# Grouped-query attention on a KV cache, one core: kv heads taken in pairs, a hand-written order, one load queue, the output weights last

## The chip, the core and the metric

The kernel runs on one NeuronCore of a Trainium2 chip. Its engines are PE (TensorE, matmuls), DVE (VectorE), ACT (ScalarE), POOL (GpSimd) and SP (SyncE, which here only issues transfers). Each runs its own instructions in order and waits for others by semaphores; 16 DMA engines move data between HBM and the on-chip memory SBUF. PE writes its results to PSUM, a memory of eight banks, from which DVE or ACT take them. The metric is device time in microseconds, the median of several runs.

## The reference

```python
B, Sq, D = 8, 4, 512
Hq, Hkv, Sk, Dh = 32, 8, 2048, 128
# x [B,Sq,D], k_cache and v_cache [B,Hkv,Sk,Dh], wq [D,Hq*Dh], wo [Hq*Dh,D], all bf16
rep = Hq // Hkv                                   # 4 query heads share a kv head
q = (x @ wq).reshape(B, Sq, Hq, Dh).transpose(0, 2, 1, 3)
k = jnp.repeat(k_cache, rep, axis=1)
v = jnp.repeat(v_cache, rep, axis=1)
scores = jnp.einsum("bhqd,bhkd->bhqk", q, k) * (Dh ** -0.5)
p = _softmax(scores, axis=-1)
o = jnp.einsum("bhqk,bhkd->bhqd", p, v)
return o.transpose(0, 2, 1, 3).reshape(B, Sq, Hq * Dh) @ wo
```

K and V are 33.55 MB each, wq and wo 4.19 MB each, x and the output 32 KB each. Every byte of K and V is used once.

## The kernel before

A *group* is one kv head of one batch: 64 groups, heads inside batches (L73). K of a group is 512 KiB and lies in SBUF as 128 partitions of 16 consecutive keys each, one row of 4 KiB per partition (`k_int`, L84 to 88); V likewise (`v_sb`, L89 to 93). K goes out on SP's queue, V on ACT's. `wo` is loaded in four pieces of 1 MiB, rows of 1 KiB, on SP's queue among the loads of groups 8, 24, 40 and 56 (L94 to 100); `wq` in four pieces ahead of all K.

For each group, PE transposes K in 16 blocks of 128 x 128 (`trans_a` L105, `trans_b` L111). The eight blocks of each half go to one PSUM tile, `kT_a` or `kT_b`, of which there is one buffer each (L49); ACT copies the first half and DVE the second into `kT_sb`. Then 16 matmuls with a block of `kT_sb` as stationary operand and the 16 queries of the group (4 heads x 4 positions) as moving operand give the scores `sT` (L154), ACT's exponential writes the probabilities `pT` (L162), 16 matmuls with V accumulate `oT_ps` (L171), one matmul of a matrix of ones with all 256 columns of `pT` gives the sums `lcs` (L179), and DVE reduces, inverts and multiplies into `oT_all` (L180 to 187). There is no maximum taken before the exponential.

The query projection (L128 to 142, 128 matmuls, 32 small ACT copies) stands ahead of the loop. For the last batch, each group is followed by the four matmuls of its heads with `wo` (L195), which accumulate `out_ps`; at the end DVE casts it and SP stores it. The code is written group by group, with K's transposition one group ahead and loads two groups ahead; a scheduler orders each engine's instructions from that, so loads run further ahead than the code has them.

Of the kernel before, what the change touches and what calls it, by code (L numbers as in the profile page):

```python
# [1 line left out]

# [7 lines left out]
BF16 = mybir.dt.bfloat16  # L10
FP32 = mybir.dt.float32
EXP = mybir.ActivationFunctionType.Exp


@with_exitstack
def kernel(
# [17 lines left out]
    NQ = rep * Sq  # L34
    KCH = Sk // 128
    DCH = D // 128
    NG = B * Hkv
    scale = float(Dh) ** -0.5
    assert Dh == 128 and Sk % 128 == 0 and D % 128 == 0
    half = Sk // 2  # L40
    hch = KCH // 2
# [4 lines left out]
    ktpool = ctx.enter_context(tc.tile_pool(name="ktpool", bufs=3))  # L46
    ppool = ctx.enter_context(tc.tile_pool(name="ppool", bufs=3))
    setup_sb = ctx.enter_context(tc.tile_pool(name="setup_sb", bufs=1))
    psum_k = ctx.enter_context(tc.tile_pool(name="psum_k", bufs=1, space=bass.MemoryType.PSUM))  # L49
    psum_s = ctx.enter_context(tc.tile_pool(name="psum_s", bufs=2, space=bass.MemoryType.PSUM))  # L50
    psum_a = ctx.enter_context(tc.tile_pool(name="psum_a", bufs=2, space=bass.MemoryType.PSUM))

    ident = const.tile([128, 128], BF16, name="ident")
    make_identity(nc, ident[:])
    ones128 = const.tile([128, 128], BF16, name="ones128")
    nc.vector.memset(ones128[:, :], 1.0)

    xT_sb = const.tile([128, DCH, T], BF16, name="xT_sb")
    qT_all = const.tile([128, B, Hq, Sq], BF16, name="qT_all")
    oT_all = const.tile([128, Hq, T], BF16, name="oT_all")  # L60
    out_sb = const.tile([T, D], BF16, name="out_sb")
    wo_sb = const.tile([128, Hq, D], BF16, name="wo_sb")
    l_bc = const.tile([128, NQ], FP32, name="l_bc")
    recip_bc = const.tile([128, NQ], FP32, name="recip_bc")

    x_sb = setup_sb.tile([T, D], BF16, name="x_sb")
    nc.sync.dma_start(x_sb[:, :], x.flatten_outer_dims())
    wq_sb = setup_sb.tile([128, DCH, HqDh], BF16, name="wq_sb")
    for dk in range(DCH):
        eng = nc.sync  # L70
        eng.dma_start(wq_sb[:, dk, :], wq[dk * 128 : (dk + 1) * 128, :])

    groups = [(b, g) for b in range(B) for g in range(Hkv)]  # L73
    woq = [int(NG * (i + 0.5) / DCH) for i in range(DCH)]

    vt = [None] * NG
    kint = [None] * NG
    kts = [None] * NG
    kta = {}
    ktb = {}  # L80

    def dma_group(gi):
        b, g = groups[gi]
        k_int = kpool.tile([128, KCH, Dh], BF16, tag="k_int", name="k_int")  # L84
        nc.sync.dma_start(
            out=k_int[:, :, :],
            in_=k_cache[b, g].rearrange("(p c) d -> p c d", c=KCH),
        )
        v_sb = vpool.tile([128, KCH, Dh], BF16, tag="v_sb", name="v_sb")  # L89
        nc.scalar.dma_start(  # L90
            out=v_sb[:, :, :],
            in_=v_cache[b, g].rearrange("(p c) d -> p c d", c=KCH),
        )
        if gi in woq:  # L94
            wi = woq.index(gi)
            hs = Hq // DCH
            nc.sync.dma_start(
                wo_sb[:, wi * hs : (wi + 1) * hs, :],
                wo[wi * hs * 128 : (wi + 1) * hs * 128, :].rearrange("(h p) j -> p h j", p=128),
            )  # L100
        kint[gi] = k_int
        vt[gi] = v_sb
        kts[gi] = ktpool.tile([128, Sk], BF16, tag="kT_sb", name="kT_sb")

    def trans_a(gi):  # L105
        ka = psum_k.tile([128, half], BF16, tag="kT_a", name="kT_a")
        for c in range(hch):
            nc.tensor.transpose(ka[:, c * 128 : (c + 1) * 128], kint[gi][:, c, :], ident[:, :])  # L108
        nc.scalar.copy(out=kts[gi][:, :half], in_=ka[:, :])  # L109

    def trans_b(gi):  # L111
        kb = psum_k.tile([128, half], BF16, tag="kT_b", name="kT_b")
        for c in range(hch):
            nc.tensor.transpose(  # L114
                kb[:, c * 128 : (c + 1) * 128], kint[gi][:, hch + c, :], ident[:, :]
            )
        nc.vector.tensor_copy(out=kts[gi][:, half:], in_=kb[:, :])  # L117

    dma_group(0)
    trans_a(0)  # L120
    trans_b(0)
    dma_group(1)

    for dk in range(DCH):
        xtp = psum_a.tile([128, T], BF16, tag="aux", name="xtp")
        nc.tensor.transpose(xtp[:, :], x_sb[:, dk * 128 : (dk + 1) * 128], ident[:T, :T])
        nc.vector.tensor_copy(out=xT_sb[:, dk, :], in_=xtp[:, :])
    for h in range(Hq):  # L128
        psq = psum_a.tile([128, T], FP32, tag="aux", name="psq")
        for dk in range(DCH):  # L130
            nc.tensor.matmul(  # L131
                psq[:, :],
                lhsT=wq_sb[:, dk, h * 128 : (h + 1) * 128],
                rhs=xT_sb[:, dk, :],
                start=(dk == 0),
                stop=(dk == DCH - 1),
            )
        nc.scalar.mul(  # L138
            out=qT_all[:, :, h, :],
            in_=psq[:, :].rearrange("d (b s) -> d b s", b=B),  # L140
            mul=scale,
        )

    out_ps = psum_a.tile([T, D], FP32, tag="outp", bufs=1, name="out_ps")

    for gi in range(NG):
        b, g = groups[gi]
        kT_sb = kts[gi]
        v_sb = vt[gi]
        q_grp = qT_all[:, b, g * rep : (g + 1) * rep, :].rearrange("d h s -> d (h s)")  # L150

        sT = psum_s.tile([128, KCH * NQ], FP32, tag="sT", name="sT")
        for c in range(KCH):
            nc.tensor.matmul(  # L154
                sT[:, c * NQ : (c + 1) * NQ],
                lhsT=kT_sb[:, c * 128 : (c + 1) * 128],
                rhs=q_grp,
                start=True,
                stop=True,
            )  # L160
        pT = ppool.tile([128, KCH * NQ], BF16, tag="pT", name="pT")
        nc.scalar.activation(out=pT[:, :], in_=sT[:, :], func=EXP)  # L162
        if gi + 2 < NG:
            dma_group(gi + 2)
        if gi + 1 < NG:
            trans_a(gi + 1)
            trans_b(gi + 1)

        oT_ps = psum_a.tile([128, NQ], FP32, tag="aux", name="oT_ps")
        for c in range(KCH):  # L170
            nc.tensor.matmul(  # L171
                oT_ps[:, :],
                lhsT=v_sb[:, c, :],
                rhs=pT[:, c * NQ : (c + 1) * NQ],
                start=(c == 0),
                stop=(c == KCH - 1),
            )
        lcs = psum_a.tile([128, KCH * NQ], FP32, tag="aux2", bufs=1, name="lcs")
        nc.tensor.matmul(lcs[:, :], lhsT=ones128[:, :], rhs=pT[:, :], start=True, stop=True)  # L179
        nc.vector.tensor_reduce(  # L180
            out=l_bc[:, :],
            in_=lcs[:, :].rearrange("p (c q) -> p q c", c=KCH),
            axis=mybir.AxisListType.X,
            op=mybir.AluOpType.add,
        )
        nc.vector.reciprocal(recip_bc[:, :], l_bc[:, :])  # L186
        nc.vector.tensor_tensor(  # L187
            out=oT_all[:, g * rep : (g + 1) * rep, b * Sq : (b + 1) * Sq],
            in0=oT_ps[:, :].rearrange("d (h s) -> d h s", h=rep),
            in1=recip_bc[:, :].rearrange("d (h s) -> d h s", h=rep),  # L190
            op=mybir.AluOpType.mult,
        )
        if b == B - 1:
            for h in range(g * rep, (g + 1) * rep):
                nc.tensor.matmul(  # L195
                    out_ps[:, :],
                    lhsT=oT_all[:, h, :],
                    rhs=wo_sb[:, h, :],
                    start=(h == 0),
                    stop=(h == Hq - 1),  # L200
                )

    nc.vector.tensor_copy(out=out_sb[:, :], in_=out_ps[:, :])
    nc.sync.dma_start(out=out.flatten_outer_dims(), in_=out_sb[:, :])

# [29 lines left out]
```

## Time and profile before

| | us |
|---|---|
| median of 3 runs | 212.43 |
| lowest and highest run | 211.34, 213.15 |
| span of the profiled execution | 210.1 |
| PE busy in it | 154.8 |
| DVE busy | 96.9 |
| ACT busy | 91.1 |

The profiled execution has its span on the page (first to last instruction) and no other time of its own; a run's time also holds what lies around the span, so spans are compared with spans and the difference to the median is added at the end. PE, DVE, ACT rows are instruction time; matmuls overlap, so PE's busy time is no sum of their lengths. The chain of waits follows the work that ended last back through what released each step:

```profile
DMA 63%; PE 24%; DVE 6%; ACT 3%; issue 2%; ACTq 1%; DVEq 0%
```

"issue" there is time in which an engine waited for nothing that the profile shows, and ACTq and DVEq are the engines' sequencers.

### The profile page before, as it was taken

To read this page: it belongs to the slowest core of one execution; us is meant where nothing else is said; L and a number is where in the kernel's file an instruction comes from. 1 tells how busy PE (TensorE), PEld (TensorE's weight loads), DVE (VectorE), ACT (ScalarE), POOL (GpSimd) and SP (SyncE) were. 2 spreads that over 40 slices of the span, in tenths; PEclk is the share of its full clock that TensorE was granted. 3 is DMA by queue.
4 is the path that set the end of the run, shared out by engine and by line. 5 is a ranking of instruction groups with operands and counts; after the bars stand their busy time and mean duration, and the time that the engine had idled before them with its cause. 6 is when DMAs were issued, how large, how long until landed. Compare 5 with 4: busy or idle time off the path is not lost.

```text
span 210.1 us, 7459 instructions
## 1 busy us (share of the span) xinstructions
PE 154.8 (74%) x3300; PEld 133.0 (63%) x3300; DVE 96.9 (46%) x262; ACT 91.1 (43%) x161; POOL 0.7 (0%) x6
## 2 busy tenths in 40 slices
PE   0000584878885877978888888898788888899981
PEld 0000574778884776968788777677777777777750
DVE  1000141235774443355665666566456665545532
ACT  0002353655352425436656555454545445664430
POOL 1000000000000000000000000000000000000000
PEclk9999996797998566589999999999699999999999
DMA  6999999999999999999999999999999999930000
GB/s 231 421 425 418 420 422 416 408 407 414 416 413 402 402 404 404 404 421 416 415 416 417 416 417 416 411 417 420 416 417 417 413 416 417 402 152 3 5 0 6
DMA packets 23296, 76.04 MB, mean 362 GB/s; under 512 B 2208, under 2 KB 6368, under 8 KB 22752
## 3 DMA queue, kind: packets, MB, share of 16 engines
q1 hardware_dynamic: 14048, 42.01, 49.8%
q10 hardware_dynamic: 9216, 33.56, 39.4%
q8 instruction: 25, 0.41, 0.7%
q14 instruction: 7, 0.06, 0.1%
HBM read 75.53 MB, written 0.03 MB: 360 GB/s over the span
## 4 chain that ended last, share of the span: by engine, by line
DMA 63%; PE 24%; DVE 6%; ACT 3%; issue 2%; ACTq 1%; DVEq 0%
DMA v_sb<-in_v_cache_dram 36%; DMA k_int<-in_k_cache_dram 21%; DMA wo_sb<-in_wo_dram 6%; PE kT_b L114 5%; PE sT L154 5%; PE kT_a L108 5%; DVE kT_sb L117 4%; PE out_ps L195 4%; PE oT_ps L171 3%; ACT pT L162 2%; ACT kT_sb L109 1%; ACTq L90 1%; PE lcs L179 1%; DVE l_bc L180 1%; DVE recip_bc L186 0%
## 5 line engine op out<-in xcount | busy, mean ns | idle before, releaser
L117 DVE COPY kT_sb<-kT_b 128x1024 bf16<-128x1024 bf16 x64 | 44.1, 689 | 77.3 <-PE kT_b L114 65.2
L109 ACT COPY kT_sb<-kT_a 128x1024 bf16<-128x1024 bf16 x64 | 64.6, 1009 | 8.4 <-PE kT_a L108 6.9
L114 PE MATMUL kT_b<-ident,k_int 128*128 128x128 bf16 x512 | 52.7, 233 | 10.9 <-DVE kT_sb L117 7.3
L162 ACT ACTIVATE pT<-sT 128x256 bf16<-128x256 f32 x64 | 24.5, 384 | 76.3 <-PE sT L154 32.3
L114 PEld LDWEIGHTS <-k_int 128*128 128x128 bf16 x512 | 38.8, 104 | 17.9 <-issue 12.6
L171 PEld LDWEIGHTS <-v_sb 128*128 128x128 bf16 x1024 | 34.7, 98 | 22.5 <-issue 22.4
L171 PE MATMUL oT_ps<-pT,v_sb 128*128 128x16 bf16 x1024 | 35.7, 170 | 16.7 <-ACT pT L162 14.8
L108 PE MATMUL kT_a<-ident,k_int 128*128 128x128 bf16 x512 | 44.9, 235 | 3.9 <-DMA k_int<-in_k_cache_dram 3.9
L180 DVE TENSOR_REDUCE l_bc<-lcs 128x16 f32<-128x256 f32 x64 | 26.9, 421 | 23.9 <-PE lcs L179 23.4
L154 PE MATMUL sT<-qT_all,kT_sb 128*128 128x16 bf16 x1024 | 37.2, 171 | 0.7 <-ACT kT_sb L109 0.4
L154 PEld LDWEIGHTS <-kT_sb 128*128 128x128 bf16 x1024 | 33.1, 98 | 6.0 <-ACT kT_sb L109 3.6
L108 PEld LDWEIGHTS <-k_int 128*128 128x128 bf16 x512 | 33.1, 105 | 4.1 <-DMA k_int<-in_k_cache_dram 4.1
L179 PE MATMUL lcs<-pT,ones 128*128 128x256 bf16 x64 | 18.4, 287 | 0.8 <-DVE oT_all L187 0.8
L131 PE MATMUL psq<-xT_sb,wq_sb 128*128 128x32 bf16 x128 | 6.7, 183 | 15.0 <-DMA wq_sb<-in_wq_dram 14.9
L186 DVE RECIPROCAL recip_bc<-l_bc 128x16 f32<-128x16 f32 x64 | 16.2, 253 | 2.2
L131 PEld LDWEIGHTS <-wq_sb 128*128 128x128 bf16 x128 | 5.5, 102 | 16.0 <-DMA wq_sb<-in_wq_dram 15.4
L187 DVE TENSOR_TENSOR oT_all<-oT_ps,recip_bc 128x16 bf16<-128x16 f32 x64 | 11.1, 174 | 3.1 <-PE oT_ps L171 0.9
L138 ACT ACT_TABLE_LOAD x1 | 1.3, 1283 | 19.7 <-DMA v_sb<-in_v_cache_dram 19.7
L195 PE MATMUL out_ps<-wo_sb,oT_all 128*32 128x512 bf16 x32 | 8.3, 382 | 1.0 <-DVE oT_all L187 1.0
L138 ACT ACTIVATE qT_all<-psq 128x32 bf16<-128x32 f32 x32 | 4.9, 202 | 7.5 <-PE psq L131 7.3
L179 PEld LDWEIGHTS <-ones 128*128 128x128 bf16 x64 | 6.2, 97 | 0.0
L195 PEld LDWEIGHTS <-oT_all 128*32 128x32 bf16 x32 | 2.4, 95 | 3.7 <-DVE oT_all L187 1.2
(11 smaller groups left out, 3.0 us busy)
## 6 DMA issues: line engine op xcount, KB each, us to landing
v_sb<-in_v_cache_dram ACTq DMA_DIRECT2D x64, 512.0 KB, 9.9
k_int<-in_k_cache_dram SPq DMA_DIRECT2D x64, 512.0 KB, 9.9
wq_sb<-in_wq_dram SPq DMA_DIRECT2D x4, 1024.0 KB, 10.3
wo_sb<-in_wo_dram SPq DMA_DIRECT2D x4, 1024.0 KB, 14.7
x_sb<-in_x_dram SPq DMA_DIRECT2D x1, 32.0 KB, 2.1
out_dram<-out_sb SPq DMA_DIRECT2D x1, 32.0 KB, 1.5
```

What stands on the lines that cost most here:

```text
L108: nc.tensor.transpose(ka[:, c * 128 : (c + 1) * 128], kint[gi][:, c, :], ident[:, :])
L109: nc.scalar.copy(out=kts[gi][:, :half], in_=ka[:, :])
L114: nc.tensor.transpose(kb[:, c * 128 : (c + 1) * 128], kint[gi][:, hch + c, :], ident[:, :])
L117: nc.vector.tensor_copy(out=kts[gi][:, half:], in_=kb[:, :])
L131: nc.tensor.matmul(psq[:, :], lhsT=wq_sb[:, dk, h * 128 : (h + 1) * 128], rhs=xT_sb[:, dk, :], start=(dk == 0), stop=(dk == DCH - 1),)
L154: nc.tensor.matmul(sT[:, c * NQ : (c + 1) * NQ], lhsT=kT_sb[:, c * 128 : (c + 1) * 128], rhs=q_grp, start=True, stop=True,)
L162: nc.scalar.activation(out=pT[:, :], in_=sT[:, :], func=EXP)
L171: nc.tensor.matmul(oT_ps[:, :], lhsT=v_sb[:, c, :], rhs=pT[:, c * NQ : (c + 1) * NQ], start=(c == 0), stop=(c == KCH - 1),)
L179: nc.tensor.matmul(lcs[:, :], lhsT=ones128[:, :], rhs=pT[:, :], start=True, stop=True)
L180: nc.vector.tensor_reduce(out=l_bc[:, :], in_=lcs[:, :].rearrange("p (c q) -> p q c", c=KCH), axis=mybir.AxisListType.X, op=mybir.AluOpTyp ...
L186: nc.vector.reciprocal(recip_bc[:, :], l_bc[:, :])
L195: nc.tensor.matmul(out_ps[:, :], lhsT=oT_all[:, h, :], rhs=wo_sb[:, h, :], start=(h == 0), stop=(h == Hq - 1),)
```

## The change

- Two kv heads of one batch make a *unit*: 32 units, pairs outermost and batches inside, so the last batch's groups are no longer the last eighth; a unit is 1 MiB of K and 1 MiB of V. Partitions 0 to 63 hold the first head and 64 to 127 the second, 32 consecutive keys each: rows of 8 KiB.
- The scores of a block have 32 columns, the queries of both heads. Only the two diagonal blocks (64 partitions x 16 columns) are meant; two exponentials write just those into `probs`, three buffers whose other entries are set to zero once at the start. The matmul with V then adds up both heads at once without mixing them.
- The work of a unit is cut in two halves of 16 blocks, each transposed in two parts of eight. `kp`, the PSUM tile of a part, has three buffers; DVE copies three parts of four, ACT the last.
- The order is written by hand (no scheduler): at each step, part 0 of the half two ahead, scores of the half one ahead, part 1, and values of this half. Sums are formed in the second half of a unit only, by 8 accumulated matmuls of 128 columns (before: one of 256 per group).
- All loads go out on SP's queue: x, wq as one transfer, then K and V of each unit, seven units in buffers, and `wo` in six pieces behind the last V. All 32 matmuls with `wo` follow the last unit.
- The projection's output is copied by 4 ACT instructions of 256 elements instead of 32 of 32.

```diff
+WO_PIECES = [(0, 8), (8, 8), (16, 8), (24, 4), (28, 2), (30, 2)]
...
-    kpool = ctx.enter_context(tc.tile_pool(name="kpool", bufs=8))
-    vpool = ctx.enter_context(tc.tile_pool(name="vpool", bufs=20))
-    psum_k = ctx.enter_context(tc.tile_pool(name="psum_k", bufs=1, space=bass.MemoryType.PSUM))
+    PRE = 7
+    kpool = ctx.enter_context(tc.tile_pool(name="kpool", bufs=PRE))
+    vpool = ctx.enter_context(tc.tile_pool(name="vpool", bufs=PRE))
+    ktpool = ctx.enter_context(tc.tile_pool(name="ktpool", bufs=6))
+    psum_k = ctx.enter_context(tc.tile_pool(name="psum_k", bufs=3, space=bass.MemoryType.PSUM))
+    psum_s = ctx.enter_context(tc.tile_pool(name="psum_s", bufs=2, space=bass.MemoryType.PSUM))
+    order = ctx.enter_context(tc.manual_schedule())
+    probs = [const.tile([128, C, NQ], BF16, name=f"probs{i}") for i in range(3)]
...
+    nc.sync.dma_start(wq_sb[:, :, :], wq.rearrange("(p r) n -> p r n", r=R))
+    units = [(p, b) for p in range(G2) for b in range(B)]
+    def load(u):
+        p, b = units[u]
+        ks[u] = kpool.tile([128, C, Dh], BF16, tag="k_sb", name="k_sb")
+        nc.sync.dma_start(
+            ks[u][:, :, :],
+            k_cache[b, 2 * p : 2 * p + 2].rearrange("g (s c) d -> (g s) c d", c=C),
+        )
...
+    for u in range(PRE):
+        load(u)
...
+    for t in probs:
+        nc.vector.memset(t[:, :, :], 0.0)
...
+    def transpose_part(i, part):
+        u, hf = divmod(i, 2)
+        c0 = hf * HC + part * (HC // 2)
+        kp = psum_k.tile([128, HC // 2, 128], BF16, tag="k", name="kp")
+        for c in range(HC // 2):
+            nc.tensor.transpose(kp[:, c, :], ks[u][:, c0 + c, :], ident[:, :])
+        k_t = ktpool.tile([128, HC // 2, 128], BF16, tag="kt", name="kt")
+        if part == 1 and hf == 1:
+            nc.scalar.copy(out=k_t[:, :, :], in_=kp[:, :, :])
+        else:
+            nc.vector.tensor_copy(out=k_t[:, :, :], in_=kp[:, :, :])
...
+    def scores(i):
...
+        for c in range(HC):
+            k_t = kt[(i, c // (HC // 2))]
+            nc.tensor.matmul(
+                s_ps[:, c, :], lhsT=k_t[:, c % (HC // 2), :], rhs=q2, start=True, stop=True
+            )
+        for g in range(2):
+            rows = slice(g * 64, (g + 1) * 64)
+            cols = slice(g * NQ // 2, (g + 1) * NQ // 2)
+            nc.scalar.activation(
+                out=pr[rows, hf * HC : (hf + 1) * HC, cols], in_=s_ps[rows, :, cols], func=EXP
+            )
...
+    def values(i):
...
+        if hf == 1:
+            l_ps = psum_l.tile([128, 4, NQ], FP32, tag="l", name="l_ps")
+            for c in range(C // 4):
+                nc.tensor.matmul(
+                    l_ps[:, :, :],
+                    lhsT=ones[:, :],
+                    rhs=pr[:, c * 4 : (c + 1) * 4, :],
+                    start=(c == 0),
+                    stop=(c == C // 4 - 1),
+                )
...
+        for c in range(HC):
+            cc = hf * HC + c
+            nc.tensor.matmul(
+                o_ps[u][:, :],
+                lhsT=vs[u][:, cc, :],
+                rhs=pr[:, cc, :],
+                start=(cc == 0),
+                stop=(cc == C - 1),
+            )
...
+    for step in range(-2, NH):
+        if step + 2 < NH:
+            transpose_part(step + 2, 0)
+        if 0 <= step + 1 < NH:
+            scores(step + 1)
+        if step + 2 < NH:
+            transpose_part(step + 2, 1)
+        if step >= 0:
+            values(step)
+            if step % 2 == 1:
+                u = step // 2 + PRE
+                if u < NU:
+                    load(u)
+                elif u == NU:
+                    for h0, n in WO_PIECES:
+                        load_wo(h0, n)
+    out_ps = psum_l.tile([T, D], FP32, tag="l", name="out_ps")
     for h in range(Hq):
...
```

SP's order of transfers from start to end, before (names as in the code; x4 and the like count equal rows in a row):

```order
L67 DMA x_sb<-in_x_dram 32x512
L71 DMA wq_sb<-in_wq_dram 128x4096 x4
L85 DMA k_int<-in_k_cache_dram 128x2048 x9
L97 DMA wo_sb<-in_wo_dram 128x8x512
L85 DMA k_int<-in_k_cache_dram 128x2048 x8
L97 DMA wo_sb<-in_wo_dram 128x8x512
L85 DMA k_int<-in_k_cache_dram 128x2048 x3
```

It goes on with two more pieces of wo and 44 loads of K; the 64 loads of V stand on ACT's queue, among its copies and exponentials. SP's end after the change, with the waits of each transfer (DMAHW0 to 7 are the semaphores that eight transfers in a row use by turns):

```order
L79 DMA k_sb<-in_k_cache_dram 128x4096 [waits DMAHW0_49]
L84 DMA v_sb<-in_v_cache_dram 128x4096 [waits DMAHW1_49,PE_49]
L90 DMA wo_sb<-in_wo_dram 128x8x512 [waits DMAHW2_49]
L90 DMA wo_sb<-in_wo_dram 128x8x512 [waits DMAHW3_49]
L90 DMA wo_sb<-in_wo_dram 128x8x512 [waits DMAHW4_49]
L90 DMA wo_sb<-in_wo_dram 128x4x512 [waits DMAHW5_49]
L90 DMA wo_sb<-in_wo_dram 128x2x512 [waits DMAHW6_49]
L90 DMA wo_sb<-in_wo_dram 128x2x512 [waits DMAHW7_49]
```

V and wo moved to SP's queue, wo behind everything else; each transfer waits for the one eight before it to land, and a V load besides for PE to be done with the unit seven before. ACT's start before (each K, V or projection row as the code names it):

```order
L90 DMA v_sb<-in_v_cache_dram 128x2048 x10
L138 ACT_TABLE_LOAD
L138 ACTIVATE qT_all<-psq 128x8x4
L109 COPY kT_sb<-kT_a 128x1024
L138 ACTIVATE qT_all<-psq 128x8x4 x2
L90 DMA v_sb<-in_v_cache_dram 128x2048
```

and after, its start up to the end of the first unit (the number behind `probs` is its buffer):

```order
L121 ACT_TABLE_LOAD
L121 ACTIVATE qT_all<-psq 128x256 x4
L156 ACTIVATE probs_93<-s_ps 64x16x16 x2
L137 COPY kt<-kp 128x1024
L156 ACTIVATE probs_93<-s_ps 64x16x16 x2
```

ACT issues no transfers any more; for two groups it had two exponentials and two copies, for a unit it has four exponentials over half the partitions and one copy.

More of the change, by code (lines that the diff above doesn't have):

```diff
@@ L64 @@
[L64 to L87, printed above, removed]
-        )
[L89 to L137, printed above, removed]
+    kpool = ctx.enter_context(tc.tile_pool(name="kpool", bufs=PRE))
@@ new lines @@
+    order = ctx.enter_context(tc.manual_schedule())
+    x_sb = const.tile([T, D], BF16, name="x_sb")
+    wq_sb = const.tile([128, R, HqDh], BF16, name="wq_sb")
+    xT_sb = const.tile([128, R, T], BF16, name="xT_sb")
+    qT_all = const.tile([128, G2, B, HP, Sq], BF16, name="qT_all")
+    oT_all = const.tile([128, Hq, B, Sq], BF16, name="oT_all")
+    wo_sb = const.tile([128, Hq, D], BF16, name="wo_sb")
+    out_sb = const.tile([T, D], BF16, name="out_sb")
+    ident = const.tile([128, 128], BF16, name="ident")
@@ L138 @@
+    for p in range(G2):
+        psq = psum_s.tile([128, HP, T], FP32, tag="s", name="psq")
+        for h in range(HP):
+            hh = p * HP + h
+            for r in range(R):
+                nc.tensor.matmul(
+                    psq[:, h, :],
+                    lhsT=wq_sb[:, r, hh * 128 : (hh + 1) * 128],
+                    rhs=xT_sb[:, r, :],
+                    start=(r == 0),
+                    stop=(r == R - 1),
+                )
         nc.scalar.mul(
-            out=qT_all[:, :, h, :],
@@ L140 @@
-            in_=psq[:, :].rearrange("d (b s) -> d b s", b=B),
+            out=qT_all[:, p, :, :, :],
+            in_=psq[:, :, :].rearrange("d h (b s) -> d b h s", b=B),
             mul=scale,
         )
[L144 to L159, printed above, removed]
-            )
[L161 to L176, printed above, removed]
-            )
[L178 to L184, printed above, removed]
-        )
[L186 to L201, printed above, removed]
@@ L203 @@
+    out_ps = psum_l.tile([T, D], FP32, tag="l", name="out_ps")
+    for h in range(Hq):
+        nc.tensor.matmul(
+            out_ps[:, :],
+            lhsT=oT_all[:, h, :, :].rearrange("d b s -> d (b s)"),
+            rhs=wo_sb[:, h, :],
+            start=(h == 0),
+            stop=(h == Hq - 1),
+        )
     nc.vector.tensor_copy(out=out_sb[:, :], in_=out_ps[:, :])
```

79 lines of the change are left out of this document (60 added, 19 removed).

## The prediction

> **What bounds the kernel now.** First the page's slices, then the window view by stage, then the chain of waits and the groups.
>
> ```profile
> span 210.1 us, 7459 instructions
> PE   0000584878885877978888888898788888899981
> PEclk9999996797998566589999999999699999999999
> DMA  6999999999999999999999999999999999930000
> GB/s 231 421 425 418 420 422 416 408 407 414 416 413 402 402 404 404 404 421 416 415 416 417 416 417 416 411 417 420 416 417 417 413 416 417 402 152 3 5 0 6
> DMA packets 23296, 76.04 MB, mean 362 GB/s; under 512 B 2208, under 2 KB 6368, under 8 KB 22752
> ```
>
> A slice is 5.25 us. All 16 DMA engines are busy from the second slice to the 35th, at 402 to 425 GB/s. The 36th slice, from 183.8 us, still moves 152 GB/s, that is 1.9 us at 416, so the loads end near 185.7 us. After that the transfers are over, and PE works on alone for 21 us. So there are two regimes: a stream of 75.5 MB that never stops, and a tail of 210.1 - 185.7 = 24.4 us without it.
>
> ```profile
> core 0: us, PE busy (x) PEld busy (x) DVE busy (x) ACT busy (x) POOL busy (x), PEclk, DMA share, GB/s
> 0.00:5.00 5.00, 0.49 (x4) 0.25 (x4) 0.68 (x5) 0.00 (x0) 0.71 (x6) 1.00 0.61 218
> 8.00:18.00 10.00, 0.70 (x6) 0.39 (x6) 0.00 (x0) 0.00 (x0) 0.00 (x0) 1.00 1.02 426
> 21.00:30.00 9.00, 6.14 (x113) 5.64 (x113) 2.66 (x5) 4.07 (x15) 0.00 (x0) 1.00 1.03 421
> 115.00:175.00 60.00, 51.20 (x1159) 44.23 (x1156) 36.02 (x94) 31.18 (x48) 0.00 (x0) 0.97 1.03 416
> 186.00:207.00 21.00, 19.20 (x321) 12.78 (x319) 9.21 (x27) 7.86 (x12) 0.00 (x0) 1.00 0.04 16
> ```
>
> ```profile
> q1 hardware_dynamic: 380, 2.85, 67.4%
> q10 hardware_dynamic: 382, 1.41, 34.4%
> ```
>
> Columns of the first: stretch, busy time of each engine, granted clock, DMA share, rate; of the second, the queues from 8 to 18 us: packets, MB, share. In the first 5 us 1.09 MB moved, 2.6 us at 421, so the stream starts in effect at 2.4 us. From 8 to 18 us two thirds of the bytes (2.85 MB, SP's queue) are wq in rows of 8 KiB and one third (1.41 MB, ACT's queue) V in rows of 4 KiB: 426. From 21 to 30 us K and V alone, 4 KiB rows: 421. In the long middle the same traffic makes 416.
>
> The tail is backlog. One group (one kv head of one batch) is 1.05 MB, 2.52 us of stream at 416; what one group costs the engines shows in the chain of waits, in a stage where data lay ready:
>
> ```profile
> 97.28 0.70 DVE kT_sb L117
> ...
> 98.02 0.38 PE kT_b L114 x4
> 98.41 0.39 PE sT L154 x16
> 98.79 0.46 PE kT_a L108 x8
> 99.25 0.24 PE kT_b L114 x4
> ...
> 99.58 0.70 DVE kT_sb L117
> ...
> 186.03 0.97 PE out_ps L195 x4
> ```
>
> Columns: start, length, work. The cycle is 2.30 us, of which 0.70 is DVE's copy out of the only kT_b buffer while PE stands. That gains only 0.2 us a group on the stream, so what was lost early (the projection waits for wq, wo's pieces lie ahead of K in SP's queue) is never made up. The first of the eight wo products of the last batch (32 matmuls, four a group) starts at 186.03: when the loads end, nearly the whole last batch is still to do.
>
> **The change, part by part.** *Bytes* stay: x, wq, K, V 71.3 MB and wo 4.19 MB. *Row size*: K and V go from 4 to 8 KiB rows, as wq has. No row shows 8 KiB rows alone. Bounds: 416 as in the middle (no gain), and 426 as in the mixed window. I take 422, the upper row less about what 4 KiB rows lost between 21 and 175 us. 71.3 MB take 169.0 us (171.4 at 416, 167.4 at 426).
>
> *One queue*: V moves from ACT's queue to SP's, so each SP load stands behind all earlier ones; nothing but loads and the output is on SP. Where SP's queue q1 ran by itself before:
>
> ```profile
> DMA packets 172, 0.63 MB, mean 418 GB/s; under 512 B 19, under 2 KB 19, under 8 KB 172
> q1 hardware_dynamic: 165, 0.61, 99.3%
> DMA packets 357, 0.39 MB, mean 387 GB/s; under 512 B 6, under 2 KB 348, under 8 KB 357
> q1 hardware_dynamic: 357, 0.39, 107.6%
> ```
>
> The first pair is 38 to 39.5 us, K with 4 KiB rows: 418 from one queue. The second is 40 to 41 us, nearly all wo in 1 KiB rows: 387. So one queue costs nothing I can size; 0 to 1% (1.7 us), and I take 0. A load needs eight loads before it landed, and a buffer seven units old: both are far behind a stream in which PE keeps up. ACT loses 64 issues, which only frees it.
>
> *wo last*: 4.19 MB at 387 are 10.9 us at the end of the stream rather than spread. The Trainium skill (DMA: Bandwidth & Descriptors, Specifications) calls transfers of 512 B and up line rate; by it wo would take 4.19 / 0.422 = 9.9 us and the sum be 1.0 us lower. The 387 beside 418 on the same queue disagrees, and the row decides.
>
> The stream's end is 2.4 + 169.0 + 10.9 = 182.3 us; the last K lands at 182.3 - 10.9 - 2.5 = 168.9, the last V at 171.4.
>
> *Does PE keep up?* Per unit (a pair of heads in one batch, 2.1 MB, 4.97 us of stream): 32 transposes at 0.46 per 8 are 1.84. Scores and values have the same number of matmuls with 32 columns for 16:
>
> ```profile
> 26.75 0.35 PE L131 MATMUL psq<-xT_sb,wq_sb 128*128 128x32 bf16 x8
> 26.96 0.54 PE L154 MATMUL sT<-qT_all,kT_sb 128*128 128x16 bf16 x16
> 100.95 0.61 PE L108 MATMUL kT_a<-ident,k_int 128*128 128x128 bf16 x8
> ```
>
> The timeline's rows hold the last one's drain, 0.17 to 0.18 us. Eight with 32 columns take 0.35, so (0.35 - 0.18)/7 = 25 ns each; sixteen with 16 take (0.54 - 0.17)/15 = 25 ns. Doubling the columns is free: 0.78 us each for scores and values. The sums of probabilities become 8 matmuls of 128 columns (one of 256 per group before): by the transposes' width 0.46. Sum 3.86 us, cover of 1.1 us a unit. The kp buffers go from one each to three, and other PE work lies between a copy and its reader, so the 0.70 us stand should go; if it stays on every second copy, 1.4 us come back and PE is late by 0.3 us a unit.
>
> The others, from the groups (mean ns is the number ahead of the second bar):
>
> ```profile
> L109 ACT COPY kT_sb<-kT_a 128x1024 bf16<-128x1024 bf16 x64 | 64.6, 1009 | 8.4 <-PE kT_a L108 6.9
> L117 DVE COPY kT_sb<-kT_b 128x1024 bf16<-128x1024 bf16 x64 | 44.1, 689 | 77.3 <-PE kT_b L114 65.2
> L162 ACT ACTIVATE pT<-sT 128x256 bf16<-128x256 f32 x64 | 24.5, 384 | 76.3 <-PE sT L154 32.3
> L180 DVE TENSOR_REDUCE l_bc<-lcs 128x16 f32<-128x256 f32 x64 | 26.9, 421 | 23.9 <-PE lcs L179 23.4
> L186 DVE RECIPROCAL recip_bc<-l_bc 128x16 f32<-128x16 f32 x64 | 16.2, 253 | 2.2
> L187 DVE TENSOR_TENSOR oT_all<-oT_ps,recip_bc 128x16 bf16<-128x16 f32 x64 | 11.1, 174 | 3.1 <-PE oT_ps L171 0.9
> ```
>
> DVE per unit: 3 x 0.689 + at most 0.421 + 0.253 + 0.174 = 2.9 us. ACT: one copy 1.009, four exponentials of 256 elements a partition (64 partitions, strided; nearest row 0.384, twice that if the stride costs) 1.54 to 3.1: 2.5 to 4.1. Both below 4.97: hidden by the stream. The three memsets and the projection come before K of unit 0 has landed, about 15 us, or beside it; PE is at most one unit late at 20 us, and 1.1 us a unit make that up.
>
> *The new tail*: after the last K two steps (3.9 us) and the last values, sums and the normalisation (about 2) end at 175 us; wo is then still landing, so the final product runs behind its pieces.
>
> ```profile
> 205.86 1.04 PE L195 MATMUL out_ps<-wo_sb,oT_all 128*32 128x512 bf16 x4 [1.01 <-DVE oT_all L187]
> 206.94 0.68 DVE L203 CAST out_sb<-out_ps 32x512 bf16<-32x512 f32 x1 [1.13 <-PE out_ps L195]
> 207.64 0.35 SPq L204 DMA_DIRECT2D out_dram<-out_sb  x1
> ```
>
> Four matmuls take 1.04 with one drain of 0.38: 0.22 each. Eight heads are 1.8 us of PE and 2.7 us of wo's stream, so PE waits for each piece; heads 16 to 23 start 2.7 us before the end of wo, and 16 matmuls of 0.22 plus drain end 1.0 us after it. From 206.9, the last matmul's end, to 210.1 were 3.2 us; they stay. Tail 4.2 for 24.4.
>
> Sum: 182.3 + 4.2 = 186.5 us of span: 20.2 less tail, 3.4 less stream (179.9 for 183.3). The runs' median, 212.43, stands 2.3 above the profiled span (1.2 to 3.0): 188.8 us.
>
> **Rivals.** *One queue falls short.* Against it is the 418 row, but it is 1.5 us long and its loads had been issued while two queues were full. If 71.3 MB go at 400: 178.3, and 198 in all; at 410: 174, 194.
>
> *The engines become the bound, still faster.* If a unit costs more than 4.97 us the stream waits for buffers. Then the time is 18 (first unit ready) + 32 units + 7.2 for the product, 1 of last values, 3.2, and 2.3: at 5.3 us a unit 201. For it: ACT's strided exponentials and copy at 4.1 are near, and the clock:
>
> ```profile
> 50.00:95.00 45.00, 36.06 (x741) 33.00 (x739) 22.77 (x65) 19.03 (x30) 0.00 (x0) 0.73 1.04 408
> ACT pT L162 <- DMA wo_sb<-in_wo_dram: 6.4, 2, 3.9
> ```
>
> Where PE was left waiting (up to 3.9 us in one wait) the granted clock fell to 0.73; 3.86/0.73 is 5.3 us a unit. Against it: with waits spread through 115 to 175 us it stayed 0.97, and the waits left here are 1.1 us. The Trainium skill (TensorE: Matmul & The Clock Gate, Part 1) asks for idle gaps over about 3.4 us before the clock drops; by that, as by the 0.97 row, this rival stays small.
>
> *Slower.* The pipeline does not overlap: PE, in its written order, stands at each copy, as at kT_b now. Serial, a unit is 4 x 0.46 + 3 x 0.69 + 1.01 + 0.78 + 0.78 + 0.46 = 6.9 us, and 32 make 252. It decides from 5.7 us a unit: 18 + 32 x 5.7 + 13.7 is over 214. Against it: three kp buffers, and scores or values of another half behind every transposition.
>
> *The change does nothing*: it would need the tail to stay, that is PE at 2.3 us a half unit with eight behind; a part of the rival above.
>
> **How the numbers follow.** Forecast 0.77, its own range 185.5 to 193 (426 or 416 for the rate, 1% for the queue, the offset 1.2 to 3.0, and a piece of wo). One queue short 0.10 (193 to 198), engines the bound but faster 0.08 (193 to 210), no change 0.01, slower 0.04. I give 185 to 198, which leaves out most of the last three and the edges. A measurement of this kernel tells about 1% from no change, the runs spread by 0.9%. Faster 0.94, same 0.02, slower 0.04.
>
> **What would show it.** Right: DMA at 9 in every slice from the second until about 182 us, 416 to 426 GB/s and 385 to 390 in the last 11 us; 8 KiB packets; PE's waits going to K's loads, up to 1.1 us a unit; clock near 1.0; the product's matmuls waiting for wo, and 4 us from the last load to the end. Wrong: slices of DMA below 9 in the middle with SP waiting on PE (the engines bind), rates near 400 with full share (the queue), or PE waiting for the kp copies.

## The result and the profile after

The changed kernel takes 195.71 us (median of 4 runs, 195.52 to 195.83), the kernel before 212.79 (211.34 to 213.25): ratio 0.9216, 95% interval 0.9177 to 0.9256. That is inside the range given, 185 to 198, but 6.9 us above the point and outside the forecast's own range, 185.5 to 193; the gain is 17.1 us where 23.6 (from 212.43) were forecast. The profiled execution took 195.7 us with a span of 193.9, so 7.4 us of span have to be explained, and the offset between span and time is 1.8 us instead of 2.3.

The page of the kernel after, to be held against the same rows before:

```profile
span 193.9 us, 7655 instructions
...
PE   1019698887788868988877878598887878877893
...
PEclk9999789999999996999999999889999999996999
DMA  6989999999999999999999999999999999999960
GB/s 223 433 382 429 414 419 428 411 422 419 411 429 407 416 424 416 421 419 414 422 416 419 421 414 422 421 416 421 417 414 419 414 421 426 411 394 320 328 208 7
DMA packets 13680, 76.05 MB, mean 392 GB/s; under 512 B 1168, under 2 KB 5328, under 8 KB 5328
...
q1 hardware_dynamic: 13648, 75.57, 95.7%
q8 instruction: 27, 0.44, 0.9%
```

A slice is now 4.85 us. The transfers fill the span nearly to its end: the tail of PE without transfers is gone. But the stream itself is no shorter. Its last load lands at 189.6 us here and at 188.5 before; what is saved is 210.1 - 188.5 = 21.6 us of tail against 193.9 - 189.6 = 4.3. The three slices before the last one, from 174.5 us, fall to 320, 328 and 208 GB/s, the first two with the engines still counted busy. The prediction's stream ends in the second of them, at 182.3 us.

The end of the chain of waits (start, length, work):

```profile
154.40 21.28 DMA k_sb<-in_k_cache_dram
175.68 0.05 issue
175.73 1.03 PE kp L134 x8
...
182.92 0.38 PE l_ps L169 x4
183.30 0.39 PE o_ps L189 x16
183.70 7.07 PE out_ps L223 x32
190.77 0.02 issue
190.79 0.68 DVE out_sb L230
```

The last K lands at 175.7; forecast was 168.9. From there it is PE work, 8.0 us to the first product and 7.1 us of products, with no wait for wo among them. The waits and the groups, for the steps on the engines:

```profile
PE kp L134 <- DMA k_sb<-in_k_cache_dram: 29.0, 28, 2.4
...
PE s_ps L150 <- ACT kt L137: 0.5, 1, 0.5
```

```profile
L156 ACT ACTIVATE probs<-s_ps 64x256 bf16<-64x256 f32 x128 | 48.3, 378 | 83.7 <-PE s_ps L150 82.1
...
L177 DVE TENSOR_REDUCE l_sb<-l_ps 128x32 f32<-128x128 f32 x32 | 9.3, 291 | 21.9 <-PE l_ps L169 21.9
```

The stages of the middle and of the first work after the last K (stretch, busy times, clock, DMA share, GB/s):

```profile
30.00:160.00 130.00, 105.24 (x2650) 102.19 (x2646) 73.63 (x154) 64.83 (x128) 0.00 (x0) 0.97 1.01 418
175.50:178.00 2.50, 2.27 (x37) 2.28 (x38) 0.69 (x1) 0.69 (x2) 0.00 (x0) 0.54 0.99 344
```

After the projection, PE waits for loads of K and for hardly anything else: the stream is the bound, as forecast. The strided exponentials cost 378 ns, the lower of the two ends given.

**Where the 6.8 us up to the last K come from.** A transfer is split over 16 DMA engines, and each adds one to the transfer's semaphore when its share has landed: the trace holds 1168 such events for 73 transfers. They carry no engine's number; an engine is meant below by the place of its share in this order. Those of one load, sorted, in us from the span's start:

```
after,  last K:   169.3 169.4 169.6 169.6 169.9 170.0 171.2 171.5 173.9 174.1 174.2 174.2 174.2 174.3 174.3 175.7
after,  last wo:  186.1 186.2 186.3 186.3 186.5 186.6 186.8 186.9 188.1 188.1 188.2 188.2 188.2 189.4 189.5 189.6
before, last load (V): 183.6 183.7 184.0 184.0 184.1 184.3 184.9 185.4 186.8 187.8 187.8 188.0 188.1 188.1 188.1 188.5
```

The fastest engine delivered its share of the last K at 169.3 us, 0.4 from the forecast 168.9. Between the first K (its first share at 15.4) and the last it moved 62 loads in 153.9 us, 2.48 us for 1.049 MB or 422 GB/s, the very rate taken. But PE waits for the slowest, which is 6.4 us later. The lag grows in steps: 1.8 us between fastest and slowest from 20 us on, 3.3 from 73, 4.9 from 124, 6.4 from 173, and between the steps it stays the same. The only traffic with such a grain are the 27 packets of 16 KiB in the row q8, the fetches of instructions, about 1.07 us each and some 6 us apart. Theory A: they fall on some of the engines only, and those lag. The rivals: some engines are slower by themselves (B), or the engines' SBUF traffic slows some transfers (C).

### The profile page after: what moved, and what is told of

Same layout as the page of the kernel before. It is cut to its first block, busy times and chain, and to the rows that moved or that the text cites. A ratio compares the mean times of both kernels' runs of the same rounds, so it can differ in the third digit from the quotient of the medians.

```text
span 193.9 us, 7655 instructions
## 1 busy us (share of the span) xinstructions
PE 146.2 (75%) x3492; PEld 137.8 (71%) x3492; DVE 95.4 (49%) x201; ACT 83.5 (43%) x165; POOL 0.7 (0%) x6
## 2 busy tenths in 40 slices
DMA packets 13680, 76.05 MB, mean 392 GB/s; under 512 B 1168, under 2 KB 5328, under 8 KB 5328
## 4 chain that ended last, share of the span: by engine, by line
DMA 88%; PE 7%; SPq 2%; ACT 1%; issue 0%; DVE 0%; ACTq 0%
DMA k_sb<-in_k_cache_dram 88%; PE out_ps L223 4%; PE kp L134 2%; SPq L79 1%; SPq L84 1%; PE s_ps L150 1%; ACT kt L137 1%; PE l_ps L169 0%; PE o_ps L189 0%; DVE out_sb L230 0%; ACTq L257 0%; SPq L70 0%; SPq L69 0%; ACT probs L156 0%; ACTq L156 0%
## 5 line engine op out<-in xcount | busy, mean ns | idle before, releaser
L134 PE MATMUL kp<-ident,k_sb 128*128 128x128 bf16 x1024 | 83.2, 228 | 29.2 <-DMA k_sb<-in_k_cache_dram 29.0
L139 DVE COPY kt<-kp 128x1024 bf16<-128x1024 bf16 x96 | 66.0, 691 | 61.8 <-PE kp L134 50.8
L134 PEld LDWEIGHTS <-k_sb 128*128 128x128 bf16 x1024 | 62.6, 102 | 32.2 <-DMA k_sb<-in_k_cache_dram 31.9
L156 ACT ACTIVATE probs<-s_ps 64x256 bf16<-64x256 f32 x128 | 48.3, 378 | 83.7 <-PE s_ps L150 82.1
L150 PE MATMUL s_ps<-qT_all,kt 128*128 128x32 bf16 x1024 | 37.1, 177 | 1.0 <-ACT kt L137 0.5
L189 PE MATMUL o_ps<-probs,v_sb 128*128 128x32 bf16 x1024 | 36.1, 177 | 0.5 <-issue 0.5
L150 PEld LDWEIGHTS <-kt 128*128 128x128 bf16 x1024 | 33.4, 97 | 1.6 <-DVE kt L139 0.7
L137 ACT COPY kt<-kp 128x1024 bf16<-128x1024 bf16 x32 | 32.4, 1012 | 0.8
L169 PE MATMUL l_ps<-probs,ones 128*128 128x128 bf16 x256 | 20.0, 219 | 0.7 <-issue 0.4
L184 DVE RECIPROCAL r_sb<-l_sb 128x32 f32<-128x32 f32 x32 | 11.3, 353 | 1.1
## 6 DMA issues: line engine op xcount, KB each, us to landing
k_sb<-in_k_cache_dram SPq DMA_DIRECT2D x32, 1024.0 KB, 19.9
v_sb<-in_v_cache_dram SPq DMA_DIRECT2D x32, 1024.0 KB, 19.9
```

Of the source, the lines that this page charges most:

```text
L134: nc.tensor.transpose(kp[:, c, :], ks[u][:, c0 + c, :], ident[:, :])
L137: nc.scalar.copy(out=k_t[:, :, :], in_=kp[:, :, :])
L139: nc.vector.tensor_copy(out=k_t[:, :, :], in_=kp[:, :, :])
L150: nc.tensor.matmul(s_ps[:, c, :], lhsT=k_t[:, c % (HC // 2), :], rhs=q2, start=True, stop=True)
L156: nc.scalar.activation(out=pr[rows, hf * HC : (hf + 1) * HC, cols], in_=s_ps[rows, :, cols], func=EXP)
L169: nc.tensor.matmul(l_ps[:, :, :], lhsT=ones[:, :], rhs=pr[:, c * 4 : (c + 1) * 4, :], start=(c == 0), stop=(c == C // 4 - 1),)
```

## The experiments

**Loads alone.** e1 keeps all transfers and their order, and drops the computation:

```diff
-    for r in range(R):
...
-    for step in range(-2, NH):
...
+    nc.vector.memset(oT_all[:, :, :, :], 0.0)
+    for u in range(NU):
+        tk = psum_k.tile([128, 128], BF16, tag="k", name="tk")
+        nc.tensor.transpose(tk[:, :], ks[u][:, 0, :], ident[:, :])
+        tv = psum_o.tile([128, 128], BF16, tag="o", name="tv")
+        nc.tensor.transpose(tv[:, :], vs[u][:, 0, :], ident[:, :])
+        if u + PRE < NU:
+            load(u + PRE)
+        elif u + PRE == NU:
+            for h0, n in WO_PIECES:
+                load_wo(h0, n)
```

> All transfers of the changed kernel in its order on its one queue; of the computation only one transposition of K and one of V per unit and the product with wo on zeros are left (projection, scores, softmax, values left out), so PE has about 200 instructions for 6986 and the instruction queue fetches next to nothing. Theory A (in the changed kernel the instruction fetches, 27 packets of 16 KiB at 1.07 us, fall on some of the 16 DMA engines only; those run 6.4 us behind the fastest at the last K, and a transfer has landed when its last engine has): the last K lands near 168 us, fastest and slowest engine under 1.5 us apart, the last wo near 180, span about 184.5. Theory B (some DMA engines are slower by themselves, whatever the engines do): last K at 175, spread 6, last wo near 189, span about 193. Theory C (SBUF traffic of PE, DVE and ACT slows some transfers): as A here, told apart by e2.

e2 adds the instructions back, without the work of the other engines:

```diff
+        dm = psum_s.tile([128, 32], FP32, tag="s", name="dm")
+        for c in range(105):
+            nc.tensor.matmul(dm[:, :], lhsT=ident[:, :], rhs=ones[:, :32], start=True, stop=True)
```

> e1 with 105 small matmuls of constants per unit on PE, so that PE again reads about as many instructions as in the changed kernel (some 6900), with no copies, exponentials or projection. Theory A: the spread between engines comes back: last K at 174 to 176 us, last wo 187 to 190, span 191 to 194. Theories B and C: nothing changes against e1 (B: both at 193; C: both near 184.5).

Measured, in one execution each: spans of 188.6 and 193.7 us. PE's timeline of e1, where the releaser in brackets is the load waited for:

```profile
170.26 0.29 PE L106 MATMUL tk<-ident,k_sb 128*128 128x128 bf16 x1 [2.20 <-DMA k_sb<-in_k_cache_dram]
172.81 0.29 PE L108 MATMUL tv<-ident,v_sb 128*128 128x128 bf16 x1 [2.26 <-DMA v_sb<-in_v_cache_dram]
175.83 9.65 PE L117 MATMUL out_ps<-wo_sb,oT_all 128*32 128x512 bf16 x32 [2.73 <-DMA wo_sb<-in_wo_dram]
```

Its stages (stretch, busy times, clock, DMA share, GB/s), the middle and wo alone:

```profile
30.00:160.00 130.00, 14.97 (x52) 5.42 (x52) 0.00 (x0) 0.00 (x0) 1.00 1.01 422
174.00:184.00 10.00, 8.17 (x26) 3.12 (x26) 0.00 (x0) 0.00 (x0) 1.00 1.08 341
```

e2's instruction queue on its page:

```profile
q8 instruction: 27, 0.44, 0.9%
```

and its middle by stages, with the loads at 419 GB/s:

```profile
30.00:160.00 130.00, 82.66 (x2702) 76.88 (x2699) 0.00 (x0) 0.00 (x0) 0.57 1.01 419
```

The last K's landings:

```
e1: 169.5 169.6 169.6 169.7 169.8 169.8 169.8 169.8 169.8 169.9 170.0 170.0 170.0 170.0 170.1 170.2
e2: 169.2 169.3 169.4 169.4 169.4 169.5 169.5 170.0 173.9 173.9 174.0 174.1 174.1 174.2 174.4 175.7
```

Without fetches (e1 has no packet of 16 KiB at all) all engines land within 0.7 us. With 27 fetches, by PE alone and with no copies, exponentials or projection, eight shares are on time and eight are 4 to 6 us late, and the last one comes at 175.7, as in the changed kernel. B falls, and so does C for the traffic of ACT and DVE. PE's own reads of SBUF came back in e2 together with the fetches, so the two runs alone do not tell these apart; the moments of the delays do. Take, for each load of e2, how far its 16 shares lie behind its fastest one, summed over the shares. This sum is 2.1 us for the load that landed at 20.9 us and 42.7 us for the last K, and 25 fetches began in between. Behind each of them it rises by 1.3 to 2.0 us (once by 2.5, over two loads), 1.6 us on average, and between them it stays within 0.4 us, though PE reads SBUF throughout (82.66 us busy of the 130). So theory A is shown: a fetch puts back one share, and the lag stays. That it is always the same eight engines is read off the split of eight and eight, since the events have no numbers. Two numbers of A were off. The rate without fetches is 422, not some 429 as the 168 us implied, so the last K of e1 lands at 170.2. And wo alone on one queue moves at 341 GB/s in this window, some 350 before its last half microsecond, in which the transfers run out, and not at 387: its last landing is at 184.7, 11.9 us after that of the last V (172.8).

**More fetches.**

> e2 with 180 small matmuls per unit for 105, 1.7 times the instructions. Theory A: about 46 fetches for 27, six or seven per fetching engine for four: the last K 3 to 4 us later than in e2, 177 to 179 us, span 194 to 198. Theories B and C: as e2.

The span was 264.9 us, in one execution, outside every theory: with 180 matmuls a unit PE itself ran out of instructions, and the loads then waited for PE.

```profile
PE dm L109 <- issue: 74.1, 36, 3.5
```

36 waits of 2.1 us on average, for 45 fetches; the first ones end some 2.4 us after the start of a packet of 16 KiB. While the stream was full, up to some 90 us, the fetches came no more often than in e2, one in 6.2 us, so the dose was the same; then the stream was no longer full, and the lag fell back (0.3 to 2 us, once 3.5). The dose could not be read. What it shows is another cost of a fetch: beside a full stream, PE can stand and wait for it.

**Two queues again.**

```diff
-        nc.sync.dma_start(
+        nc.scalar.dma_start(
             vs[u][:, :, :],
```

> The changed kernel with the loads of V issued from ACT again, K, wq and wo from SP; all else the same. Theory A and the prediction's zero for one queue: the loads' rate does not change (418 +- 2 GB/s in the middle), the time stays within 2 us of the changed kernel's 195.7. Rival (one queue is what gains: V's transfers beside wq delay the projection to about 22 us, and ACT's exponentials stand behind its own transfers' waits): 199 us or more, with waits of ACT on transfers.

208.45 us, 12.7 more than the changed kernel: the rival holds. The rate in the middle is the same, so the gain of the one queue is not in the stream:

```profile
30.00:160.00 130.00, 103.11 (x2545) 99.84 (x2542) 69.23 (x147) 61.37 (x122) 0.00 (x0) 0.95 1.01 418
```

ACT's timeline:

```profile
54.60 1.01 ACT L137 COPY kt<-kp 128x1024 bf16<-128x1024 bf16 x1
64.68 0.34 ACTq L84 DMA_DIRECT2D v_sb<-in_v_cache_dram  x1
65.12 1.59 ACT L156 ACTIVATE probs<-s_ps 64x256 bf16<-64x256 f32 x4 [9.51 <-issue]
```

The exponentials stand for 9.5 us behind a load of V that ACT cannot issue yet; PE waits for them, and the projection, too, began 5.0 us later (18.6 for 13.7), the first transposition 6.5. Neither is ever made up, and the reason is in the chain of waits, where PE is the bound:

```profile
142.84 1.44 issue
144.28 0.48 PE o_ps L189 x13
...
149.31 1.44 issue
150.75 0.48 PE s_ps L150 x13
151.23 0.46 PE kp L134 x8
...
155.88 1.07 issue
```

The sums of two units with no such stop between them, from DVE's timeline:

```profile
157.43 0.29 DVE L177 TENSOR_REDUCE l_sb<-l_ps 128x32 f32<-128x128 f32 x1 [1.83 <-PE l_ps L169]
...
161.26 0.29 DVE L177 TENSOR_REDUCE l_sb<-l_ps 128x32 f32<-128x128 f32 x1 [0.60 <-PE l_ps L169]
```

3.83 us a unit, where 3.86 were forecast. But a unit has 208 instructions on PE, a fetch brings some 259 (6986 rows in 27 fetches), and when PE is never waiting for data it stands 0.9 to 1.4 us for each (from 120 to 156 us); these stops begin 1.0 to 1.4 us after the start of a packet of 16 KiB. From 66.6 to 193.0 us 25 units took 5.06 us each, more than the stream's 4.97: there is no cover, and a delay stays to the end. How much of the 12.7 us is the late start and how much the 9.5 us was not separated.

**wo ahead of the last four units.**

```diff
+                if u == NU - 4:
+                    for h0, n in WO_PIECES:
+                        load_wo(h0, n)
                 if u < NU:
                     load(u)
-                elif u == NU:
-                    for h0, n in WO_PIECES:
-                        load_wo(h0, n)
```

> The changed kernel with wo's six pieces ahead of the last four units instead of behind the last V; all else the same. Theory A (what follows the last K is one chain on PE: 8.0 us to the first product, 7.1 us of products, 3.2 us to the end; wo behind it is what covers that chain): the last K lands 11.4 us later, near 187, and the span ends at 187 + 8.0 + 7.1 + 3.2 = 205, the time is 207. Rival (the same bytes, the same time): within 2 us of 195.7.

206.9 us, span 205.4, and from the last K to the end, in the chain of waits, the same steps as in the changed kernel:

```profile
187.40 1.04 PE kp L134 x8
...
195.16 7.07 PE out_ps L223 x32
```

So 11.2 us are what wo's place at the end is worth: PE's chain runs while wo lands.

**Rows of 4 KiB.**

```diff
+        for c0 in (0, HC):
             nc.sync.dma_start(
-                ks[u][:, :, :],
-                k_cache[b, 2 * p : 2 * p + 2].rearrange("g (s c) d -> (g s) c d", c=C),
+                ks[u][:, c0 : c0 + HC, :],
+                k_cache[...].rearrange("g (s c) d -> (g s) c d", c=C)[:, c0 : c0 + HC, :],
...
```

(`k_cache[...]` stands for the same index as before; V is cut likewise.)

> The changed kernel with each load of K and V as two transfers of 512 KiB with rows of 4 KiB for one of 1 MiB with rows of 8 KiB. The prediction took 422 GB/s for 8 KiB and 416 for 4 KiB: 415 to 417 in the middle for 418, the last K 1 to 2.5 us later, 196.5 to 198.5. Rival (row size is worth nothing here, the rate is that of the stream with its fetches): the same within 0.5 us.

200.5 us, 4.8 more, where at most 2.8 were expected. The middle:

```profile
30.00:160.00 130.00, 101.62 (x2584) 99.02 (x2582) 71.80 (x149) 62.70 (x124) 0.00 (x0) 0.97 1.03 407
```

407 GB/s for 418. The edit halves the transfers along with the rows, and with them what is under way: a load lands 10.2 us after its issue, in the changed kernel 19.9. So which of these costs the rate is open. The kernel before had 416 in its long middle with the same row size and size of transfer, on two queues, and its loads landed 9.9 us after their issue. By this comparison of two different kernels, small rows and transfers on one queue are slower than on two, while with the large ones it makes no difference (418 in the changed kernel and in e4); no run has the kernel after with small rows on two queues.

**Fewer instructions, and a shorter chain.** e7 forms the sums with 2 matmuls of 512 columns for 8 of 128; e8 adds that the first eight heads' product stands ahead of the last values, and wq comes in four transfers; e10 is e8 without the split of wq, and the last heads' pieces of wo go out from SP and ACT by turns.

```diff
-            for c in range(C // 4):
+            for c in range(2):
...
-                    rhs=pr[:, c * 4 : (c + 1) * 4, :],
+                    rhs=pr[:, c * HC : (c + 1) * HC, :],
...
+        if step == NH - 2:
+            out_ps = psum_k.tile([T, D], FP32, tag="k", name="out_ps")
+            project(0, 8)
```

> The changed kernel with the sums formed by 2 matmuls of 512 columns per unit for 8 of 128 (and DVE reducing 16 columns for 4): 6602 rows on PE for 6986, all else the same. Theory A (fetches set the lag): some 25 fetches for 27, further apart; the fourth on the slowest engine, at 171 us before, falls behind the last K, which lands near 174.3 for 175.7; wo still ends near 189.6, so the span falls by 0.5 to 1: 194.7 to 195.2. Rival (no link between instructions and landing in the whole kernel): the last K at 175.7, 195.5 to 196 or, by DVE's longer reduction at the end, later.

> e7 with two more edits: the first eight heads' product stands ahead of the last two halves' values, the others behind them as before, so that PE's last chain is some 1.8 us shorter; and wq comes as four transfers with rows of 8 KiB for one with 32 KiB. Theory A (both chains matter: PE's after the last K, and wo's last landing plus 0.6 and 3.1 us): the end is then wo's alone; with 0.5 us from wq (rate 420 for 382 in the second slice) the last wo lands at 189, the span is 192.5 to 193, the time 194.2 to 194.9. Rival (PE's chain is what sets the end): 1.8 us from the product's move alone, 193.5 or less.

> e8 with wq as one transfer again, and the last heads' pieces of wo issued by turns from SP and from ACT (ACT's behind the exponentials of the last unit's first half). Theory (with 1 KiB rows one queue gives 348 GB/s as in e1, two give more; the fast engines are held back by one queue's order): wo's end 1 to 1.5 us earlier, the time 193.8 to 194.6. Rival (the slowest engine's lag sets the end, the queue does not matter): 195 to 195.6. If ACT's last copy stands behind a transfer's wait: later than 196.

Measured: 195.33 us (195.01 to 196.41, ratio 0.9184, 0.9135 to 0.9233), 195.48 (195.20 to 195.76) and 195.85 (195.72 to 196.48). None can be told from the changed kernel's 0.9216. In e7 the fetches are 25, and the last K lands at 174.3 us as theory A has it; the step that came at 173 before now comes during wo, and the last wo lands at 189.1. In e8 the last product waits for wo:

```profile
184.13 1.89 PE L207 MATMUL out_ps<-wo_sb,oT_all 128*32 128x512 bf16 x8 [1.13 <-DMA wo_sb<-in_wo_dram]
186.89 3.61 PE L207 MATMUL out_ps<-wo_sb,oT_all 128*32 128x512 bf16 x16 [0.88 <-DMA wo_sb<-in_wo_dram]
```

So PE's chain and wo's landing on the slowest engine end within 0.6 us of each other in the changed kernel, and shortening one brings up the other. wq in four transfers gave nothing, since the first two slices lost (186 and 424 GB/s for 223 and 433) what the third gained (422 for 382). In e10 the last wo lands at 189.5, as in e8, and wo's rate from 176 to 182 us is 344 GB/s: the second queue brings nothing. Its issues cost a little: three of them took ACT 1.5 us, and PE waited 1.81 us for ACT's last copy, 0.49 in e8.

**The buffers of kp.**

```diff
-    psum_k = ctx.enter_context(tc.tile_pool(name="psum_k", bufs=3, space=bass.MemoryType.PSUM))
+    psum_k = ctx.enter_context(tc.tile_pool(name="psum_k", bufs=1, space=bass.MemoryType.PSUM))
```

> The changed kernel with one buffer of the transposition tile kp for three. The prediction let the wait of PE for its copy go because of the three buffers. Theory A (that wait is what the third buffer removes, and PE has little to spare, since each fetch stops it for up to 1.4 us when it is never waiting for data): each of four parts a unit waits 0.3 to 1.0 us, a unit costs PE 5.5 to 6 us for 3.83, the engines bind: 205 to 225 us. Rival (1.1 us of cover a unit suffices, the stream binds anyway): 195.5 to 198.

> The changed kernel with two buffers of kp for three. Between the writing of a part and of the one after the next lie a copy and two other blocks of PE work, so PE should wait little: 195.5 to 197 by both theories; over 198 would say that the order needs all three.

224.83 us with one buffer, slower than the kernel before, and 195.73 with two. With one, PE's waits are

```profile
PE kp L134 <- DVE kt L139: 41.0, 96, 0.9
...
PE kp L134 <- ACT kt L137: 8.2, 28, 1.1
```

and a unit takes 5.94 us. That is the place of the prediction's slower rival, at the price it named (slower from 5.7 us a unit), reached by taking away what stood against it. And the tail is back: the last load lands at 193.6 us, 29 us before the end of the span (222.8). Two buffers are enough.

## Why the prediction was right, and where it was off

- *The range.* That 195.7 us lies in it is in part luck. The forecast's own range ended at 193; up to 198 it was drawn out for the rival in which one queue falls short, at 400 to 410 GB/s, and that did not happen (418). Two of the signs named for the forecast did not come either: no matmul of the product waited for wo, and the last 11 us of the loads had 328 GB/s and less instead of 385 to 390.
- *The tail was the backlog, and it goes.* Right: after the last landing 4.3 us are left where 21.6 were (the page's rates had put the loads' end at 185.7 and the tail at 24.4, but the last share landed at 188.5). It comes back where PE falls behind: 18.0 us in e4, 29 in e9. That 4.3 is so close to the 4.2 forecast is chance: the product was to end behind wo's last piece, and what it ended behind was PE's own late chain.
- *The rate of 8 KiB rows, 422.* Right, for the shares that no fetch delays, and in e1 for all.
- *The stream's end at 182.3 us.* This is the step that failed. It took one rate of the 16 engines together for the landing of a transfer, and a transfer has landed when its slowest engine has. The instruction fetches fall on half of the engines (e1 against e2), and the last share of the last K came 6.4 us after the first. The kernel before shows the same lag, 4.9 us at its end, so it could have been read there.
- *wo at 387.* Taken from one microsecond in which wo followed K; alone it is some 350 in e1, where wo takes 11.9 us instead of 10.9 (4.19 MB at 387 are 10.8). In the changed kernel it took 11.4 from the last V's last landing (178.2) to its own, half a microsecond more than forecast. The rule of the Trainium skill (DMA: Bandwidth & Descriptors, Specifications) that 512 B and more go at line rate does not hold here for wo's rows of 1 KiB: some 350 beside 422 for rows of 8 KiB.
- *The sum of it*: 0.4 late at the fastest engine, 6.4 for the slowest, 0.5 for wo make 7.3 us, the end of the loads at 189.6 for 182.3. With 0.1 of tail, and 0.5 less between span and time, that is the 6.9 us.
- *PE's chain after the last K.* Forecast 6.1 us, took 8.0: the granted clock was 0.54 between 175.5 and 178 us, after PE had waited, and the scores stood for ACT's copy. In the changed kernel this chain ends last, but only 0.6 us behind what wo's landing allows, so a shorter one gains next to nothing (e8).
- *One queue costs nothing.* Right with rows of 8 KiB and transfers of 1 MiB (e4: 418 on two queues as on one). With rows of 4 KiB in transfers of 512 KiB the rate was the rival's, 407 (e6), though the time, 200.5, was above its 193 to 198. What one queue gains is on ACT, which no longer stands behind its own loads (e4); the prediction had no term for that.
- *PE keeps up with 1.1 us of cover.* The work was right, 3.83 for 3.86. The cover was not: a PE that has fallen behind needs 5.06 us a unit, fetches included (e4). The changed kernel is saved from that by never falling behind, since it waits for K 28 times, 29.0 us in all. That the next fetch comes in during these waits fits its short waits of the kind "issue" (0.5 us at most), and is not shown beyond that.
- *The wait at kp's copy goes with the buffers.* Right; two of the three do it, and with one the time is 224.83 us (e9).
- *The clock.* Right for the mean: 0.97 from 30 to 160 us. But it was granted at half in four stretches of 3.4 us, from 22.1, 73.3, 124.5 and 175.7 us, each beside a wait of PE for K (1.7, 2.4, 2.4 and 1.8 us); the last three waits are those in which the lag takes a step. The Trainium skill (TensorE: Matmul & The Clock Gate, Part 1) has it drop after idle gaps of over some 3.4 us; here shorter ones went with a drop. The wait of 3.9 us that the prediction set beside the clock of 0.73 was ACT's; PE's longest in that stretch was 2.2.

## What to carry to other kernels

When a kernel is bound by a full stream of loads, ask when the slowest DMA engine delivers, not what the 16 move on average: compare the first and the last of a transfer's 16 landings, and count instruction fetches as traffic, which here fell on half of the engines. Put behind the last critical load what needs no long chain after it, and keep transfers off the queue of an engine on whose arithmetic others wait. An engine whose work per step is only a little below the stream's must never be delayed, since it has nothing to make the delay up with.

## What the runs showed of the hardware that was not expected

- Instruction fetches delay the data on some of the 16 DMA engines, by the landings on eight of them: 27 packets of 16 KiB for some 7000 rows of PE, 1.07 us each. In e2 each put back a load under way by 1.6 us on average, summed over its shares, and the lag was not made up until the stream's end.
- Beside a full stream PE stands for instructions when nothing else stops it: 0.9 to 1.4 us per fetch in e4 from 120 to 156 us, 2.1 us in e3.
- While wo's rows of 1 KiB follow loads with lagging engines, the fast engines are held back: in the changed kernel two of wo's pieces took the fastest engine 4.2 us each, from 174.6 to 183.1, and the slowest 2.9 to 3.0, and the lag shrank from 6.4 to 3.5 us. The cause is open: e10, with two queues at the end, gained nothing.
- 407 GB/s for rows of 4 KiB in transfers of 512 KiB on one queue (e6), 416 on two (the kernel before), 418 for rows of 8 KiB in transfers of 1 MiB on either (the changed kernel and e4).
